# The first batch's 4x4 pixel sums as TensorE products with a matrix of ones

## The chip, the core and the metric

The kernel runs on one core of one Trainium2 chip. The metric is the device time of one execution in microseconds (us), as the median of several runs. The core has a matrix engine (TensorE, PE in the profile; its loads of weights have a row of their own, PEld), three engines for element-wise work (VectorE or DVE, ScalarE or ACT, GpSimd or POOL), and SyncE (SP), which here issues all DMAs.

## The reference

Two batches of keys and values come as images of 384 x 32 pixels with 128 channels. Windows of 4 x 4 pixels are averaged to 768 tokens a batch, which one 128 x 128 matrix projects; the result is both keys and values. Each of 2 x 12288 queries attends to its batch's 768 tokens, and the output goes through two MLPs of width 2048.

```python
kv_pool = kv.reshape(B, H // r, r, W // r, r, C).mean(axis=(2, 4))   # r = 4
kv_flat = kv_pool.reshape(B, -1, C) @ w_sr
k = v = kv_flat
s = scale * (q @ k.transpose(0, 2, 1))
s = s - s.max(-1, keepdims=True)
a = np.exp(s)
a /= a.sum(-1, keepdims=True) + 1e-09
x = a @ v                                  # attention
x = (h * cos(h)) @ w_out1                  # h = x @ w_in1
x = (g * sigmoid(1.702 * g)) @ w_out2      # g = x @ w_in2
```

## The kernel before

Queries go in units of 512 tokens (48 of them, in groups of 16), four steps of 128 tokens to a unit. For a group the attention steps come first, then the steps of the first MLP, then those of the second. The program is written out by hand: `at(step, rank, fn)` puts work into a step, and each engine runs its instructions in the order in which they are written. Nothing reorders them between engines; an engine waits on semaphores.

The change touches what stands ahead of the first step. SP issues the load of `w_sr`, then the keys of batch 0: six blocks j, each of four loads r (`kv_load`, L117 to L124), 24 loads of 256 KB, then two units of q (L304), then eight pieces of the first MLP's weights (L194). At most eight loads are under way; each further issue waits for the one eight before it.

Block j is 16 window rows of 8 windows: 128 windows, one on each partition. Load r brings pixel row r of every window, 4 pixels x 128 channels, 2 KB a partition. A load thus takes every fourth pixel row of 64, 16 pieces of 16 KB each.

`kv_pool` (L126 to L145) sums the 16 pixels of a window by halving adds over the free axis: three of 512 wide, one of 256, one of 128. GpSimd does blocks 0 and 3, VectorE 1, 2, 4 and 5 (L557 to L568). `kv_project` (L147 to L182) then takes half a batch, three blocks, in three stages. `turn` transposes the pooled blocks on TensorE (L155) into PSUM, and ScalarE copies them out with the factor 1/16 (L157). `keys` multiplies by `w_sr` (L161), and ScalarE and VectorE write the product as a high and a low part (L163, L164). `values` does the same the other way round (L176, L179, L180). `q_prep(0)` transposes the first queries (L312 to L317); it is called behind `turn` of the second half, ahead of that half's `keys`. The first scores (L345) need the keys of both halves and the queries.

Products of plain float32, as L161 and L176, are two instructions to a call, each with its load of weights; transposes and the products of the main loops (fp32r, L102 to L104, L345, L400) are one. In TensorE's rows the first operand to be held still is called the weights; the other one streams through.

Of the kernel before, what the change touches and what calls it, by code (L numbers as in the profile page):

```python
# [11 lines left out]
F32 = mybir.dt.float32  # L12
# [4 lines left out]
ALU = mybir.AluOpType  # L17
AX = mybir.AxisListType

P = 128  # L20
# [12 lines left out]
def tile_pooled_attention_two_mlps(  # L33
# [11 lines left out]
    nc = tc.nc  # L45
    B, N, C = q.shape
# [23 lines left out]
    make_identity(nc, ident)  # L70
    wsr = cp.tile([P, C], F32, tag="wsr", name="wsr")
    wi, wo = [None, None], [None, None]
    kT = [cp.tile([P, 2, 2, HK], F32R, tag=f"kT{b}", name=f"kT{b}") for b in range(B)]
# [10 lines left out]
    def acc(key=None):  # L84
        """The bank used longest ago; a key holds it until let_go."""
        a = banks.pop(0)
        if key is None:
            banks.append(a)
        else:
            held[key] = a  # L90
        return a
# [13 lines left out]

# [1 line left out]
    pooled, staged = {}, {}  # L107
    peak = cp.tile([P, 2 * B], F32, tag="peak", name="peak")

    def kv_place(b, j):  # L110
        """Two places' worth where each of three weights goes later."""
        if j % 2 == 0:
            tag = ("wi1", "wo1", "wo0")[j // 2]
            staged[b, tag] = cp.tile([P, 2, R, R * C], F32, tag=tag, name=f"kv{b}_{j}")
        return staged[b, ("wi1", "wo1", "wo0")[j // 2]][:, j % 2]

    def kv_load(b, j):  # L117
        t = staged[b, j] = kv_place(b, j)
        hh = P // (W // R)
        src = kv[b, j * hh * R : (j + 1) * hh * R].rearrange(  # L120
            "(h r) (w s) c -> r h w (s c)", r=R, s=R
        )
        for r in range(R):
            nc.sync.dma_start(t[:, r, :], src[r])  # L124

    def kv_pool(b, j, eng):  # L126
        """The sums over a tile's windows, as short operations."""
        f = staged.pop((b, j)).rearrange("p r x -> p (r x)")
        n = R * R * C // 2
        ops = []  # L130

        def add(o, x, y):
            ops.append(lambda: eng.tensor_tensor(o, x, y, op=ALU.add))

        while n > C:
            for i in range(0, n, UNIT):
                e = min(i + UNIT, n)
                add(f[:, i:e], f[:, i:e], f[:, n + i : n + e])
            n //= 2
        pj = f[:, :C]  # L140
        if j >= 4:
            pj = st.tile([P, C], F32, tag="pooled", name=f"pooled{b}_{j}", bufs=2)
        pooled[b, j] = pj
        add(pj, f[:, :n], f[:, n : 2 * n])
        return ops  # L145

    def kv_project(b, h):  # L147
        """Half of a batch's keys and values, as stages."""
        js = range(h * KC // 2, (h + 1) * KC // 2)
        v = {}  # L150

        def turn():
            tp = acc()
            for i, j in enumerate(js):
                nc.tensor.transpose(tp[:, i * P : (i + 1) * P], pooled.pop((b, j)), ident)  # L155
            pT = v["pT"] = fp.tile([P, HK], F32, tag="f", name=f"pT{b}_{h}")
            nc.scalar.activation(pT, tp[:, :HK], AF.Copy, scale=1.0 / (R * R))  # L157
# [25 lines left out]

# [1 line left out]
    PIECE = DFF // 8  # L185
# [17 lines left out]
    def w_split(m, part, k, raw):  # L203
        """Float32 words, then their two parts."""
        d = wi[m] if part == 0 else wo[m].rearrange("p h k c -> p h (k c)")
# [3 lines left out]
        def words(stage):  # L209
# [7 lines left out]
            w = v["w"] = word.bitcast(F32)  # L217
            # Sign and upper exponent bit keep their places; seven exponent bits and twenty
            # mantissa bits move up by three, and the lower word's upper bits follow.
            if stage == 0:  # L220
                nc.vector.tensor_scalar(
                    word, high, 3, 0x3FFFFFFF, op0=ALU.logical_shift_left, op1=ALU.bitwise_and
                )
                nc.vector.scalar_tensor_tensor(
                    word, high, 0xC0000000, word, op0=ALU.bitwise_and, op1=ALU.bitwise_or
                )
            elif stage == 1:
                nc.vector.scalar_tensor_tensor(  # L228
                    word, low, 29, word, op0=ALU.logical_shift_right, op1=ALU.bitwise_or
                )  # L230
                nc.vector.tensor_scalar(
                    high, high, 1, 28, op0=ALU.logical_shift_left, op1=ALU.logical_shift_right
                )
            else:
                # What lies below float32's normal range is zero.
                nc.vector.scalar_tensor_tensor(w, high, 7.0, w, op0=ALU.is_ge, op1=ALU.mult)
# [13 lines left out]
    def w_bound(flags):  # L250
        """1 where no |h| of the first MLP can come near pi / 2: |x_c| <= max |v_c|; as stages."""
        mags = [t.rearrange("p i x -> p (i x)") for t in parts_ring]
# [29 lines left out]

    # What outlives a branch stays in places of its own, used in turn.
    def ring(n, shape, dtype, name):
# [7 lines left out]

# [1 line left out]
    qn, qT = {}, {}  # L294
# [23 lines left out]

# [1 line left out]
    tasks = defaultdict(list)  # L320
# [15 lines left out]
    def attn_step(s, u, t):  # L336
# [53 lines left out]
        def pv(part):  # L390
# [10 lines left out]
            if t == QT - 1 and part == len(PV_CUTS) - 2:  # L401
                # Before the branch the scalar engine goes on to the next stage at once.
                if u != GROUP - 1:
                    keep(u)
# [31 lines left out]
    def mlp_step(s, m, u, p):  # L436
# [7 lines left out]
        def nonlinear():  # L444
# [7 lines left out]
            else:  # L452
                # Two parts of two pi, the first one's products exact; the ends as Sin takes them.
                k = fp.tile([P, 2, UNIT], I32, tag="f", name=f"k{u}_{p}")
# [71 lines left out]

    nc.vector.memset(half_pi, math.pi / 2)
    first = GROUP * QT
    eased = set()
# [13 lines left out]
    with tc.manual_schedule():  # L543
# [12 lines left out]

        def pool_now(j, eng):  # L557
            for op in kv_pool(0, j, eng):
                op()

        pool_now(0, nc.gpsimd)
        pool_now(1, nc.vector)
        pool_now(2, nc.vector)
        half0[0]()
        pool_now(3, nc.gpsimd)
        half0[1]()
        pool_now(4, nc.vector)
        pool_now(5, nc.vector)  # L568
        half0[2]()
        half1[0]()  # L570
        q_prep(0)
        half1[1]()
        half1[2]()
        late = [*range(4, KC), *range(4)]
        # Steps that don't also split queries on the same engine.
        free = [x for x in range(6, first) if x % QT != 1]
# [22 lines left out]
        for fn, step in zip(stages, (41, 42, 43, 44, 46, 47)):  # L599
            at(step, 58, fn)  # L600
        # The second MLP's inputs take the places of the first one's.
        x_ring = ring(GROUP, [P, UNIT], F32, "x")
        # Products of the next stage, where this one's last steps wait for each other.
        for i, rank in enumerate((21, 21, 70)):
# [57 lines left out]
```

## Time and profile before

| | us |
|---|---|
| median of 3 runs | 2772.45 |
| lowest and highest | 2771.88, 2774.81 |
| span of the profiled execution | 2771.1 |
| TensorE busy in it | 2733.8 (99%) |
| VectorE busy | 1914.3 (69%) |
| ScalarE busy | 2046.8 (74%) |
| GpSimd busy | 525.5 (19%) |

The profiled execution has its span alone on the page, from its first to its last instruction; the runs' times hold what lies around it too, 1.35 us by the median. Busy time counts an instruction from start to end; TensorE's instructions overlap, and their ends are modelled. A chain of waits is followed back from the last instruction, at each step to what released it. A wait that a row names in brackets is the idle time ahead of the instruction and what ended it.

### The profile page before, as it was taken

What the parts mean: (1) busy time and instruction counts of PE and PEld (TensorE: products, weight loads), DVE (VectorE), ACT (ScalarE), POOL (GpSimd) and SP (SyncE); (2) the same over time, 40 slices, a digit from 0 to 9 for tenths busy, and PEclk for the clock granted to TensorE, in tenths of its full rate; (3) what the DMA queues carried; (4) which work ended last, traced back from release to release, by engine and by line L of the source; (5) the groups of instructions that cost most, each with busy time, mean ns of one, the idle gap of its engine ahead of it and who ended that gap; (6) DMA issues with size and microseconds to landing.
All of it is one profiled execution on the core that took longest, in us unless ns stands there. A gap on an engine that the chain in (4) does not pass through costs nothing.

```text
span 2771.1 us, 35036 instructions
## 1 busy us (share of the span) xinstructions
PE 2733.8 (99%) x13680; PEld 2310.2 (83%) x13680; DVE 1914.3 (69%) x2201; ACT 2046.8 (74%) x2455; POOL 525.5 (19%) x430
## 2 busy tenths in 40 slices
PE   6999999999999999999999999999999999999999
PEld 5998888888888899888888888889998888888887
DVE  6988999864444577788886444457778888644444
ACT  4777888777777777777777777777777777777776
POOL 5852232000000144200000000014420000000000
PEclk9999999999999999999999999999999999999999
DMA  7210000000000000000000000000000000000000
GB/s 206 69 40 15 20 20 8 1 1 13 15 12 12 22 26 24 5 1 1 1 1 1 12 12 12 12 20 30 22 1 1 1 1 1 1 12 12 12 12 17
DMA packets 27710, 48.53 MB, mean 18 GB/s; under 512 B 2832, under 2 KB 7056, under 8 KB 27536
## 3 DMA queue, kind: packets, MB, share of 16 engines
q1 hardware_dynamic: 27536, 46.21, 5.3%
q8 instruction: 109, 1.79, 0.3%
q14 instruction: 65, 0.53, 0.1%
HBM read 33.62 MB, written 12.58 MB: 17 GB/s over the span
## 4 chain that ended last, share of the span: by engine, by line
PE 92%; DVE 6%; DMA 1%; ACT 0%; issue 0%; POOL 0%; SPq 0%; DVEq 0%; POOLq 0%; ACTq 0%
PE w L103 12%; PE w L102 12%; PE w L104 12%; PE a L102 12%; PE a L103 12%; PE a L104 12%; PE a L400 7%; PE w L345 7%; PE w L370 4%; DVE g L461 2%; DVE gs L468 2%; PE a L502 1%; DMA kv<-in_kv_dram 1%; PE a L312 1%; DVE wt L228 1%; DVE nm L352 0%
## 5 line engine op out<-in xcount | busy, mean ns | idle before, releaser
L468 DVE TENSOR_TENSOR gs<-g,gs 128x1024 fp32r<-128x1024 f32 x752 | 923.5, 1228 | 565.0 <-ACT gs L466 565.0
L466 ACT ACTIVATE gs<-g 128x1024 fp32r<-128x1024 f32 x768 | 807.0, 1051 | 4.0 <-PE a L104 2.5
L448 ACT ACTIVATE g<-w 128x1024 f32<-128x1024 f32 x384 | 394.1, 1026 | 300.7 <-PE w L104 300.7
L102 PE MATMUL w<-xs,wi 128*128 128x512 f32 x1536 | 613.1, 399 | 0.0
L103 PE MATMUL w<-xs,wi 128*128 128x512 f32 x1536 | 608.1, 396 | 0.0
L104 PE MATMUL w<-xs,wi 128*128 128x512 f32 x1536 | 607.5, 395 | 0.0
L103 PE MATMUL a<-gs,wo 128*128 128x512 f32 x1536 | 606.3, 395 | 0.0
L102 PE MATMUL a<-gs,wo 128*128 128x512 f32 x1536 | 604.8, 394 | 1.0 <-DVE gs L468 1.0
L104 PE MATMUL a<-gs,wo 128*128 128x512 f32 x1536 | 597.8, 389 | 0.0
L451 ACT ACTIVATE g<-w,half_pi 128x1024 f32<-128x1024 f32 x384 | 430.1, 1120 | 219.4 <-PE w L104 218.9
L461 DVE TENSOR_TENSOR g<-w,g 128x1024 f32<-128x1024 f32 x384 | 469.1, 1222 | 134.1 <-ACT g L451 134.0
L334 POOL TENSOR_TENSOR xs<-x,xs 128x512 fp32r<-128x512 f32 x96 | 176.5, 1839 | 1692.4 <-ACT xs L333 1601.2
L102 PEld LDWEIGHTS a<-gs,wo 128*128 128x128 f32 x1536 | 288.5, 188 | 72.9 <-DVE gs L468 2.3
L104 PEld LDWEIGHTS w<-xs,wi 128*128 128x128 f32 x1536 | 288.3, 188 | 70.8
L104 PEld LDWEIGHTS a<-gs,wo 128*128 128x128 f32 x1536 | 288.7, 188 | 66.6
L102 PEld LDWEIGHTS w<-xs,wi 128*128 128x128 f32 x1536 | 288.4, 188 | 66.9 <-DVE pT L388 0.4
L103 PEld LDWEIGHTS a<-gs,wo 128*128 128x128 f32 x1536 | 288.3, 188 | 65.5
L103 PEld LDWEIGHTS w<-xs,wi 128*128 128x128 f32 x1536 | 288.8, 188 | 62.2
L388 DVE TENSOR_TENSOR pT<-w,pT 128x768 fp32r<-128x768 f32 x192 | 183.6, 956 | 110.3 <-ACT pT L385 110.0
L385 ACT ACTIVATE pT<-w 128x768 fp32r<-128x768 f32 x192 | 156.2, 814 | 133.8 <-PE w L370 129.6
L345 PE MATMUL w<-kT,qT 128*128 128x384 f32 x1152 | 250.4, 353 | 1.3 <-DVE pT L388 1.3
L365 POOL TENSOR_SCALAR e<-e,rs 128x768 f32<-128x768 f32 x192 | 182.6, 951 | 348.2 <-DVE rs L364 190.1
(67 smaller groups left out, 2091.0 us busy)
## 6 DMA issues: line engine op xcount, KB each, us to landing
kv<-in_kv_dram SPq DMA_DIRECT2D x48, 256.0 KB, 4.9
qn<-in_q_dram SPq DMA_DIRECT2D x48, 256.0 KB, 2.6
out_dram<-r SPq DMA_DIRECT2D x48, 256.0 KB, 2.0
raw<-in_moe_w_in_dram SPq DMA_DIRECT2D x16, 256.0 KB, 4.5
raw<-in_moe_w_out_dram SPq DMA_DIRECT2D x16, 256.0 KB, 2.6
wsr<-in_w_sr_dram SPq DMA_DIRECT2D x1, 64.0 KB, 1.8
```

Of the source, the lines that this page charges most:

```text
L102: nc.tensor.matmul(o, wh, xl, start=start, stop=False)
L103: nc.tensor.matmul(o, wh, xh, start=False, stop=False)
L104: nc.tensor.matmul(o, wl, xh, start=False, stop=stop)
L345: nc.tensor.matmul(sc[:, h, :HK], w, kT[b][:, i, h], start=w is qh and i == 1, stop=w is ql,)
L365: nc.gpsimd.tensor_scalar(e, e, rs, 1.0, op0=ALU.mult, op1=ALU.mult)
L388: nc.vector.tensor_tensor(v["lo"], v["src"], f32(v["hi"]), op=ALU.subtract)
L400: nc.tensor.matmul(o, w, x, start=k == 0, stop=k == n - 1)
L448: nc.scalar.activation(g, h, AF.Gelu_apprx_sigmoid)
L451: nc.scalar.activation(g, h, AF.Sin, bias=half_pi)
L461: nc.vector.tensor_tensor(g, h, g, op=ALU.mult)
L466: nc.scalar.activation(gs[:, 0], g, AF.Copy)
L468: eng.tensor_tensor(gs[:, 1], g, f32(gs[:, 0]), op=ALU.subtract)
```

## The change

Batch 0's keys are loaded in another shape: load d (of 24) now takes 16 whole pixel rows, 256 KB that lie together. A partition (x, w) holds four neighbouring pixels of pixel row x, those of window w. So the 128 partitions of a load are 16 pixel rows x 8 windows across, which is 4 window rows of 8 windows, 32 windows.

`window` is a 128 x 32 matrix with a one where partition (x, w) belongs to the window: VectorE makes it from the identity by one reduction. `kv_sum` multiplies, for each of the four neighbouring pixels, the pixels (as weights, 128 partitions x 128 channels) by `window` and accumulates the four products in 32 columns of PSUM. These columns hold channels x windows, already turned, so batch 0 has no transposes any more and no adds. `kv_project(0, h)` calls it for 12 loads in `turn`. The second half's `turn` is now called behind `q_prep(0)`. Batch 1 is loaded and pooled as before.

```diff
+    window = cp.tile([P, P // R], F32, tag="window", name="window")
     def kv_load(b, j):
         t = staged[b, j] = kv_place(b, j)
+        if b == 0:
+            rows = kv[b].rearrange("(d x) (w s) c -> d x w (s c)", x=R * R, s=R)
+            for r in range(R):
+                nc.sync.dma_start(t[:, r, :], rows[j * R + r])
+            return
+    def kv_sum(h, d, a):
+        j, r = divmod(d, R)
+        f = staged[0, j][:, r, :]
+        n = P // R
+        o = a[:, (d - h * HK // n) * n :][:, :n]
+        for i in range(R):
+            nc.tensor.matmul(
+                o, f[:, i * C : (i + 1) * C], window, start=i == 0, stop=i == R - 1
+            )
         def turn():
             tp = acc()
-            for i, j in enumerate(js):
-                nc.tensor.transpose(tp[:, i * P : (i + 1) * P], pooled.pop((b, j)), ident)
+            if b == 0:
+                for d in range(js.start * R, js.stop * R):
+                    kv_sum(h, d, tp)
+            else:
+                for i, j in enumerate(js):
+                    nc.tensor.transpose(tp[:, i * P : (i + 1) * P], pooled.pop((b, j)), ident)
     nc.vector.memset(half_pi, math.pi / 2)
+    nc.vector.tensor_reduce(
+        window, ident.rearrange("p (h r w) -> p h w r", h=R, r=R), axis=AX.X, op=ALU.add
+    )
-        pool_now(0, nc.gpsimd)
-        pool_now(1, nc.vector)
-        pool_now(2, nc.vector)
         half0[0]()
-        pool_now(3, nc.gpsimd)
         half0[1]()
-        pool_now(4, nc.vector)
-        pool_now(5, nc.vector)
         half0[2]()
-        half1[0]()
         q_prep(0)
-        half1[1]()
-        half1[2]()
+        for stage in half1:
+            stage()
```

On TensorE, from its first instruction to the first scores, the order before is this. A row is the kernel's line, the instruction with what it writes and reads, the size, and how many calls follow each other; `kv_0`, `kv_2` and `kv_4` are blocks 0 and 1, 2 and 3, 4 and 5, `a_86` and `a_87` two banks of PSUM, and `qn_95` the first queries.

```order
L155 MATMUL a_86<-ident,kv_0_103 128x128 x2
L155 MATMUL a_86<-ident,kv_2_112 128x128
L161 MATMUL a_87<-pT_0_166,wsr 128x384
L176 MATMUL a_86<-wsr,pT_0_166 128x128 x3
L155 MATMUL a_87<-ident,kv_2_112 128x128
L155 MATMUL a_87<-ident,pooled_4_177 128x128
L155 MATMUL a_87<-ident,pooled_5_183 128x128
L312 MATMUL a_86<-ident,qn_95 128x128 x4
L161 MATMUL a_87<-pT_1_197,wsr 128x384
L176 MATMUL a_86<-wsr,pT_1_197 128x128 x3
L345 MATMUL w_83<-kT_79,qT_89 128x384 x6
```

The order after, at the same place. The lines are those of the changed kernel: L161 is now `kv_sum`, L183 and L198 the products of keys and values, L334 the queries' transposes, L367 the scores; the banks are `a_87` and `a_88`, the first queries `qn_96`.

```order
L161 MATMUL a_87<-window,kv_0_105 128x32 x32
L161 MATMUL a_87<-window,kv_2_114 128x32 x16
L183 MATMUL a_88<-pT_0_198,wsr 128x384
L198 MATMUL a_87<-wsr,pT_0_198 128x128 x3
L334 MATMUL a_88<-ident,qn_96 128x128 x4
L161 MATMUL a_87<-window,kv_2_114 128x32 x16
L161 MATMUL a_87<-window,kv_4_123 128x32 x32
L183 MATMUL a_88<-pT_1_265,wsr 128x384
L198 MATMUL a_87<-wsr,pT_1_265 128x128 x3
L367 MATMUL w_84<-kT_80,qT_90 128x384 x6
```

The three transposes of each half have become 48 sums, and the queries' transposes have moved from behind the second half's blocks to ahead of them.

On VectorE, from the start to the first scores' maximum, before:

```order
L527 MEMSET half_pi 128x1
L133 TENSOR_TENSOR kv_0_103<-kv_0_103 128x512 x3
L133 TENSOR_TENSOR kv_0_103<-kv_0_103 128x256
L133 TENSOR_TENSOR kv_0_103<-kv_0_103 128x128
L133 TENSOR_TENSOR kv_2_112<-kv_2_112 128x512 x3
L133 TENSOR_TENSOR kv_2_112<-kv_2_112 128x256
L133 TENSOR_TENSOR kv_2_112<-kv_2_112 128x128
L164 SCALAR_TENSOR_TENSOR kT_79<-a_87,kT_79 128x384
L167 TENSOR_REDUCE peak<-a_87 128x1
L133 TENSOR_TENSOR kv_4_121<-kv_4_121 128x512 x3
L133 TENSOR_TENSOR kv_4_121<-kv_4_121 128x256
L133 TENSOR_TENSOR pooled_4_177<-kv_4_121 128x128
```

And after, where L186, L189 and L202 are the low part of the keys, their peak and the low part of the values, and L374 the scores' maximum:

```order
L549 MEMSET half_pi 128x1
L550 TENSOR_REDUCE window<-ident 128x32
L186 SCALAR_TENSOR_TENSOR kT_80<-a_88,kT_80 128x384
L189 TENSOR_REDUCE peak<-a_88 128x1
L202 TENSOR_TENSOR vN_82<-a_87,vN_82 128x384
L186 SCALAR_TENSOR_TENSOR kT_80<-a_88,kT_80 128x384
L189 TENSOR_REDUCE peak<-a_88 128x1
L202 TENSOR_TENSOR vN_82<-a_87,vN_82 128x384
L374 TENSOR_REDUCE nm_0_308<-w_84 128x1
```

All adds (L133) are gone from this stretch, the reduction that makes `window` has come in, and the first values' low part (L180 before, where it stood behind the last of the adds) now follows the keys' peak.

## Rows read from the trace of the kernel before

**Rows 1.** The page: busy time and share of the span by engine; the last chain by engine.

```profile
PE 2733.8 (99%) x13680; PEld 2310.2 (83%) x13680; DVE 1914.3 (69%) x2201; ACT 2046.8 (74%) x2455; POOL 525.5 (19%) x430
...
PE 92%; DVE 6%; DMA 1%; ACT 0%; issue 0%; POOL 0%; SPq 0%; DVEq 0%; POOLq 0%; ACTq 0%
```

**Rows 2.** The chain of waits up to 75 us: start, length, what; longest pieces.

```profile
26.93 0.70 DVE kv L133
...
28.85 0.30 DVE pooled L133
...
29.20 0.47 PE a L155
29.67 1.11 PE a L312 x4
...
33.60 2.91 PE w L345 x12
...
45.56 1.05 PE w L345 x6
```

**Rows 3.** Groups by line and shape up to 31 us, of VectorE and of GpSimd.

```profile
L133 DVE TENSOR_TENSOR kv<-kv 128x512 f32<-128x512 f32 x12 | 9.0, 754 | 11.8 <-DMA kv<-in_kv_dram 11.5
...
L133 POOL TENSOR_TENSOR kv<-kv 128x512 f32<-128x512 f32 x6 | 7.5, 1260 | 11.4 <-DMA kv<-in_kv_dram 11.2
```

**Rows 4.** Timeline of TensorE: start, length from first start to last end, line, count.

```profile
18.76 1.65 PE L161 MATMUL a<-pT,wsr 128*128 128x384 f32 x2 [0.58 <-ACT pT L157]
20.20 1.49 PE L176 MATMUL a<-wsr,pT 128*128 128x128 f32 x6
24.27 0.47 PE L155 MATMUL a<-ident,kv 128*128 128x128 f32 x1 [2.58 <-POOL kv L133]
...
139.27 0.83 PE L176 MATMUL a<-wsr,pT 128*128 128x128 f32 x6
```

**Rows 5.** One line each: count, shortest, median and longest ns; 0 to 34 us, then later.

```profile
L161 PE MATMUL a<-pT,wsr x4: 847/848/1007, 18.8 to 31.2; 128*128 128x384 f32 x4
...
L176 PEld LDWEIGHTS a<-wsr,pT x12: 286/333/337, 19.6 to 33.0; 128*128 128x128 f32 x12
L176 PE MATMUL a<-wsr,pT x12: 421/421/580, 20.2 to 33.2; 128*128 128x128 f32 x12
...
L345 PE MATMUL w<-kT,qT x7: 333/338/443, 35.0 to 36.2; 128*128 128x384 f32 x7
...
L176 PEld LDWEIGHTS a<-wsr,pT x12: 187/192/192, 139.1 to 152.9; 128*128 128x128 f32 x12
L176 PE MATMUL a<-wsr,pT x12: 270/275/275, 139.3 to 153.0; 128*128 128x128 f32 x12
...
L269 PEld LDWEIGHTS a<-xs,vr x4: 80/81/82, 159.1 to 172.4; 128*2 128x2 f32 x4
...
L370 PE MATMUL w<-ident,e x339: 270/273/329, 59.8 to 228.0; 128*128 128x128 f32 x170
...
L102 PE MATMUL a<-gs,wo x48: 389/393/497, 2701.5 to 2764.1; 128*128 128x512 f32 x48
```

**Rows 6.** Stretches: busy time and count by engine, granted clock, DMA share, GB/s.

```profile
10.00:25.00 15.00, 4.82 (x12) 2.75 (x12) 9.63 (x16) 1.47 (x3) 8.36 (x8) 1.00 1.07 276
27.00:33.00 6.00, 3.81 (x12) 2.48 (x13) 2.88 (x6) 2.06 (x4) 1.02 (x1) 1.00 1.05 385
```

**Rows 7.** Us to landing of the first 24 key loads, then the first q loads (L304).

```profile
DMA to landing us min/median/max: 3.6/7.2/7.7
...
L304 SPq DMA_DIRECT2D qn<-in_q_dram x2: 334/336/337, 20.1 to 21.1; - x2
...
DMA to landing us min/median/max: 7.0/7.1/7.2
```

**Rows 8.** Timeline of ScalarE and of VectorE behind the mark.

```profile
29.70 0.49 ACT L157 ACTIVATE pT<-a 128x384 f32<-128x384 f32 x1 [7.49 <-PE a L155]
...
32.62 0.56 DVE L164 SCALAR_TENSOR_TENSOR kT<-a,kT 128x384 fp32r<-128x384 f32 x1 [3.01 <-ACT kT L163]
```

More of the change, by code (lines that the diff above doesn't have):

```diff
@@ L555, in tile_pooled_attention_two_mlps @@
         half0, half1 = kv_project(0, 0), kv_project(0, 1)
-        def pool_now(j, eng):
-            for op in kv_pool(0, j, eng):
-                op()
-        pool_now(0, nc.gpsimd)
-        pool_now(1, nc.vector)
-        pool_now(2, nc.vector)
         half0[0]()
-        pool_now(3, nc.gpsimd)
         half0[1]()
-        pool_now(4, nc.vector)
-        pool_now(5, nc.vector)
         half0[2]()
-        half1[0]()
         q_prep(0)
-        half1[1]()
-        half1[2]()
+        for stage in half1:
+            stage()
         late = [*range(4, KC), *range(4)]
```

## The prediction

> **What bounds the kernel now.** I read the page first: TensorE is busy 99% of the span and carries 92% of the chain that ended last [rows 1]. Behind the start lies one TensorE-bound stream, so a change at the start counts by when that stream begins and by nothing else. So I read next the chain of waits over the first 40 us [rows 2]. Up to 26.93 it is the DMA of batch 0's keys. Then come the last adds on VectorE, the last transpose at 29.20, the queries' transposes from 29.67, key and value products, and the scores from 33.60. I call 29.67, when the last pooled block has left TensorE, the **mark**. The question is where the mark goes and what follows it.
>
> **What is removed.** In the first 31 us VectorE makes 12 adds of 754 ns over 128x512, GpSimd 6 of 1260 ns [rows 3], with 14 smaller ones between them. Nearly all lie beside the DMA. On the path lie those after 26.93, until 29.15, and one transpose of 0.47 [rows 2]. If the DMA stays as it is, 29.67 - 26.93 = 2.7 us is all that can be won here.
>
> **What is added outside TensorE.** One VectorE reduction makes the matrix of ones, once. It reads 128x128 elements; an add over 128x512 takes 0.75 us [rows 3], so it takes less. It stands second on VectorE, and no key lands before 1.17 + 3.6 = 4.8 us at today's pace [rows 7]: nothing. Without that cover it would cost up to 0.75.
>
> **What is added on TensorE.** 24 loads of 4 pixels each make 96 calls. One call in float32 is two loads of weights and two products (the one call of L161 at 18.76 shows as x2, the three of L176 as x6 [rows 4]); so 192 pairs, 96 in each half. The pixels are the weights (128 columns), the ones stream through them (32 columns).
>
> No row has a pair with 32 streaming columns. The nearest is L176 with 128: early six take 1.49 us, one alone 0.421, (1.49 - 0.42) / 5 = 0.213 us a pair; near 139 us six take 0.83, one 0.275: 0.111 a pair [rows 4, 5]. These are the clock's two levels, 1.2 and 2.4 GHz. The granted clock reads 1.00 early too [rows 6], so in these first microseconds the durations are the witness. Load and product are equally wide there, so this row doesn't tell which sets the pace. Two others do: a load of 128 columns takes 188 ns fast, one of 2 columns 81 [rows 5], and the difference, 107, is nearly the whole fast pair; and a product of L102 that finds its load not yet made takes 497 instead of 393, 104 more [rows 5]. So the load sets it, and shrinking the product frees nothing. I take **0.213 us slow, 0.111 fast**. Bounds of the slow price: above, load and product in series, 0.213 + 0.213 / 4 = 0.267; below, the first product of L161 waits 1007 - 847 = 160 ns for its load [rows 5]; and lowest, if the clock were no matter to loads, the fast 0.111.
>
> The Trainium skill, page "TensorE: Matmul & The Clock Gate", section "LDWEIGHTS (loading the stationary operand)", gives a load its columns divided by 1.2, which is 107 ns for 128, and doesn't ask for the clock. The trace speaks against it: the same loads take 333 ns early and 192 late [rows 5]. By the page the sum below would end at about 2774 with the faster key loads.
>
> **What is moved.** TensorE runs in order. Its order is now: 12 loads' sums, the first half's keys and values, *the queries' transposes*, and only then the second half's 12 loads. So half the pairs stand behind the whole first half and behind q's landing: q is issued at 20.1 and lands 7.0 to 7.2 later, at 27.2 [rows 7]. On VectorE the first values' low part no longer stands behind two tiles of adds; nobody waited for it. On SP the order of issues is the same, but batch 1's first eight loads, which go where blocks 4 and 5 were, now wait for the last sums, and a q load stands behind them that is needed a stage later. That wait moves with the scores: no price of its own.
>
> **The loads themselves.** Each now reads one contiguous 256 KB, as the q loads do. Key loads move 276 GB/s (10 to 25 us), q and weight loads 385 (27 to 33) [rows 6]. If the shape is the reason, 256 KB take 0.68 us instead of 0.95, and q lands at 4.5 + 24 x 0.68 = 20.8. In my sum this is hidden: TensorE is later than either. First landing: 4.8 [rows 7] at today's shape, 4.5 taken.
>
> **The sum, slow clock.** Half 0: 4.5 + 96 x 0.213 = 24.9, with the first load and the drain 25.2. ScalarE's copy 0.53 with its start [rows 8], load 0.16, keys 2 x 0.64 = 1.28, values 6 x 0.213 = 1.28: 28.5. Queries 4 x 0.213 = 0.85: 29.3. Half 1: 96 x 0.213 = 20.4, drain 0.2: mark at **50.0**, 20.3 later. From the mark to the scores it was 33.60 - 29.67 = 3.9; without the queries it is copy 0.53, keys 0.16 + 1.28 + 0.21, copy 0.53, low part 0.63 [rows 8]: 3.4. Net 20.3 - 0.5 = +19.8. The profiled execution spans 2771.1; the runs' median is 2772.45, the 1.35 outside the span stay. 2772.45 + 19.8 = **2792**.
>
> **Rivals.**
> *A: the clock rises during the sums, and the loads are faster.* For it: TensorE is then fed without a gap, and an uninterrupted feed from 29.67 [rows 2] had L345 at its fast 338 ns from 35.25 on [rows 5], 5.6 us later. Against it: there 128 to 384 columns streamed each time; here the array streams for a quarter of each pair. And the feed of 18.76 to 21.69 did not raise it: the next transpose took 0.47, against 0.273 fast [rows 4, 5]. The time: 5.6 us do 26 pairs, 70 x 0.111 = 7.8, half 0 ends at 18.0, values at 20.0, q lands at 20.8, its transposes 0.45, 96 x 0.111 = 10.7: mark 32.1. On to the scores at fast durations (copies 0.53 twice, load 0.11, keys 0.64 + 0.2, low part 0.63) 2.6 instead of 3.9, and the first twelve score products 2.1 instead of 2.9 (six fast take 1.05 [rows 2]): 2.4 - 1.3 - 0.8 = +0.3, **2773**. The same page of the Trainium skill, Part 1 ("The HAM clock gate"), says that sustained matmul activity releases the clock; if these sums are such activity, it is this rival. No row of before shows whether they are.
> *B: the clock rises, the loads stay as they are.* q lands at 27.2, TensorE idles 7 us and is slow again: 28.1 + 5.6 + 7.8 = mark 41.5, scores at 44.1, less 0.8: +9.7, **2782**.
> *C: slow clock, cheaper loads of weights.* At 0.160 half 0 ends at 20.2, the queries at 24.3 to 28.1, mark 39.9 to 43.6, scores 43.3 to 47.0: +9.7 to +13.4, **2782 to 2786**. At 0.111: values 18.7, queries 21.7 to 28.1, mark 32.5 to 38.9, +2.3 to +8.7, **2775 to 2781**.
> *D: pairs in series.* 192 x 0.054 = 10.4 more: **2803**.
> *E: faster.* The sums' loads go at the price of a transpose's load: a fast transpose that finds it not yet made takes 329 instead of 273 ns [rows 5], 0.056. With fast clock and fast loads half 1 is 96 x 0.056 = 5.4 behind 21.3: mark 26.8, -2.9 - 1.3 - 0.8 = -5.0, **2767**. It begins to win from a pair of about 0.107 down and needs all three; the 104 ns of L102 speak against it.
> That the change doesn't do what it says is excluded by the order: the 96 calls are there, the adds are gone.
>
> **How the numbers follow.** Chances: forecast 0.46; A 0.23; B 0.07; C 0.09 and 0.05; D 0.06; E 0.04. Below about 0.2% (5.5 us) a measurement of this kernel can't tell a change. Slower: 0.46 + 0.07 + 0.09 + 0.06 and a part of C's cheaper price, 0.70. Same: A, the rest of that price, some of E, 0.27. Faster: the rest of E, 0.03. The forecast alone is good to 4 us (first landing 1, pair price 2, the clock's rise behind the mark 1): 2788 to 2796. The range reaches down to A, 2771 to 2796; D, E and A's lower edge are left out.
>
> **What would show it.** The sums' pairs 0.21 us apart (0.11: A); the queries' transposes near 29 (21: A); key loads at 385 or 276 GB/s; the last sum's end near 50, the scores from 53. An end of the sums before 35 makes the clock or the load's price wrong, one after 55 the overlap. If the mark comes as forecast and the end isn't 20 us later, the stream behind it had slack that the chain of waits doesn't show.

## The result and the profile after

The changed kernel takes 2789.78 us (median of 5 runs, 2788.25 to 2790.8), the kernel before 2773.96 in the same comparison (2771.88 to 2774.81): ratio 1.0061, 95% interval 1.0048 to 1.0073. It is slower by 16 us, and lies inside the range, 2 us from the forecast.

The page after, beside [rows 1]: the line of busy time by engine.

```profile
PE 2770.8 (99%) x13866; PEld 2349.4 (84%) x13866; DVE 1901.1 (68%) x2182; ACT 2047.5 (73%) x2455; POOL 516.7 (19%) x420
```

TensorE is still busy 99% of the span, of a span 17.6 us longer (2788.7 against 2771.1). It has 186 instructions more (192 products came, 6 transposes went) and is busy 37 us longer. VectorE and GpSimd have lost 13.2 and 8.8 us of work, of which only the last adds, 26.93 to 29.15 [rows 2], had been waited for.

The chain of waits after, over the first 70 us (start, length, what), to be read beside [rows 2]:

```profile
1.18 2.85 DMA kv<-in_kv_dram
...
4.17 20.67 PE a L161 x96
...
25.41 1.65 PE a L183 x2
...
27.05 1.28 PE a L198 x6
...
28.73 1.09 PE a L334 x4
29.82 20.38 PE a L161 x96
...
53.70 2.90 PE w L367 x12
```

The DMA is on it for the first load only. From 4.17 on TensorE is the chain: 96 pairs, the first half's keys and values, the queries, 96 pairs, then the scores at 53.70 where [rows 2] had them at 33.60. The mark is at 50.20. (A chain has an instruction begin where the one before it ends, a timeline has its own start: the first scores stand at 53.70 in the one and at 53.35 in the other.) Before, the DMA set the start, with TensorE busy 5.3 of the first 27 us; after, TensorE does, and the DMA engines are nearly idle by then (a share of 0.05 from 30 to 50 us).

The groups by line and shape over the first 52 us (count | busy us, mean ns of one | idle before):

```profile
L161 PE MATMUL a<-window,kv 128*128 128x32 f32 x192 | 41.2, 400 | 4.2 <-DMA kv<-in_kv_dram 4.2
L161 PEld LDWEIGHTS a<-window,kv 128*128 128x128 f32 x192 | 41.1, 333 | 4.2 <-issue 4.1
```

A load of weights takes 333 ns, as the early loads of L176 did by their median [rows 5], though a quarter of the columns stream here. The pair's pace is (20.67 - 0.40) / 95 = 0.213 us. The loads follow each other without a gap (PEld is busy 10.00 of 10.00 us in the next row).

A stretch of the trace after (from:to and length, busy time and count of PE, PEld, DVE, ACT, POOL, then granted clock, DMA share, GB/s), beside [rows 6]:

```profile
10.00:20.00 10.00, 10.00 (x49) 10.00 (x48) 0.00 (x0) 0.00 (x0) 0.00 (x0) 1.00 1.05 389
```

Key loads now move 389 GB/s instead of 276. The granted clock reads 1.00 here, as it does early in the trace of before, where loads of the same length ran; so the durations are the witness, and they are those of the 1.2 GHz level. The record first shows a change of the clock at 35.2 us before and at 55.3 after.

### The profile page after: what moved, and what is told of

Same layout as the page of the kernel before. It is cut to its first block, busy times and chain, and to the rows that moved or that the text cites. A ratio compares the mean times of both kernels' runs of the same rounds, so it can differ in the third digit from the quotient of the medians.

```text
span 2788.7 us, 35369 instructions
## 1 busy us (share of the span) xinstructions
PE 2770.8 (99%) x13866; PEld 2349.4 (84%) x13866; DVE 1901.1 (68%) x2182; ACT 2047.5 (73%) x2455; POOL 516.7 (19%) x420
## 4 chain that ended last, share of the span: by engine, by line
PE 94%; DVE 5%; ACT 0%; POOL 0%; issue 0%; DMA 0%; SPq 0%; POOLq 0%; DVEq 0%; ACTq 0%
PE w L103 12%; PE w L104 12%; PE w L105 12%; PE a L103 12%; PE a L104 12%; PE a L105 12%; PE a L422 7%; PE w L367 7%; PE w L392 4%; PE a L161 1%; DVE g L483 1%; DVE gs L490 1%; PE a L524 1%; PE a L334 1%; DVE wt L250 1%
## 5 line engine op out<-in xcount | busy, mean ns | idle before, releaser
L367 PE MATMUL w<-kT,qT 128*128 128x384 f32 x1152 | 249.5, 352 | 0.0
```

Source lines behind the costliest of these rows:

```text
L367: nc.tensor.matmul(sc[:, h, :HK], w, kT[b][:, i, h], start=w is qh and i == 1, stop=w is ql,)
```

## The experiments

The theory: the cost is the weight loads' price at the slow clock, 192 x 0.213 us, of which 20 us lie on the path. The rivals: the order (queries ahead of the second half), the clock alone, the loads' new shape. All kernels below are the changed kernel with the edit that is shown; `...` stands for code left out. A time from one run alone is called so, and there the trace carries the argument. The kernel before, run beside them, had medians of 2772.2 to 2772.8 us.

### The old order

```diff
+        half1[0]()
         q_prep(0)
-        for stage in half1:
-            stage()
+        half1[1]()
+        half1[2]()
```

> The queries' transposes go back behind the second half's sums, as in the kernel before; nothing else differs. Theory (192 pairs at 0.213 one behind the other set the start, wherever q stands): the second half's sums start near 28.4 instead of 29.6 and end near 49, the queries' transposes then lie ahead of the keys, the scores come within 1 us of 53.3 and the time stays within 2 us of 2790. Rival (what costs is that the second half was put behind q): back to about 2774.

2790.34 us (one run). Its timeline of TensorE (start, length, line, count, idle before):

```profile
28.60 20.69 PE L161 MATMUL a<-window,kv 128*128 128x32 f32 x96 [0.35 <-DVE peak L189]
49.10 1.09 PE L334 MATMUL a<-ident,qn 128*128 128x128 f32 x4
```

The second half begins 1 us earlier and the scores come at 52.68 instead of 53.35. The order costs a microsecond at most; it is not the cause.

### Half the products

```diff
-        for i in range(R):
+        for i in range(2):
...
-                o, f[:, i * C : (i + 1) * C], window, start=i == 0, stop=i == R - 1
+                o, f[:, i * C : (i + 1) * C], window, start=i == 0, stop=i == 1
```

> Only two of the four pixels of each row are multiplied: 48 pairs a half instead of 96; half of each sum is left out. Theory: each half's sums take 10.2 us instead of 20.5; the first ends near 14.5, the queries wait for q until about 21.5, the second half runs from 22.3 to 32.7: 17.5 us earlier than with all pixels, the time near 2772. Rival (the stream behind the start has slack that swallows most of the delay): much less than 15 us gained.

2773.33 us, ratio 1.0002 (0.9993 to 1.0011). TensorE's timeline:

```profile
3.99 10.57 PE L161 MATMUL a<-window,kv 128*128 128x32 f32 x48 [3.99 <-DMA kv<-in_kv_dram]
...
21.31 1.08 PE L334 MATMUL a<-ident,qn 128*128 128x128 f32 x4 [3.24 <-DMA qn<-in_q_dram]
22.19 10.29 PE L161 MATMUL a<-window,kv 128*128 128x32 f32 x48
```

Half the pairs take half the time, 10.4 us a half. The kernel's time is back at that of the kernel before, so the loss goes with the number of pairs. What is new is the wait of 3.24 us for q: with less work ahead of it, the order of the changed kernel begins to cost.

### The clock: ones repeated to 128 columns

```diff
-    window = cp.tile([P, P // R], F32, tag="window", name="window")
+    window = cp.tile([P, P], F32, tag="window", name="window")
-        o = a[:, (d - h * HK // n) * n :][:, :n]
+        o = a[:, (d - h * HK // n) * n :][:, :P]
```

The reduction that makes `window` is made four times, side by side. Each product now writes 128 columns of PSUM, and the 96 that are too many are written over by the next loads' sums or not read.

> The ones are repeated to 128 columns, so each product streams 128 columns instead of 32; the pixels' loads of weights stay as they are. Theory (a pair costs its load of weights, 0.213 us at the slow clock, and the clock stays slow because the array streams only a quarter of the time): the pairs begin at 0.213 as before, load and product being equally wide, but the array now streams without a gap, so some 5.6 us after the first sum the pairs fall to 0.111, the last sum ends near 32 instead of 50 and the time is near 2772. Rival (the clock doesn't rise for such sums however wide they stream): 0.213 throughout, 2790. Rival (product and load one after the other): the pairs get longer, to 0.37, and the time goes above 2815.

2775.12 us, ratio 1.0009 (1.0000 to 1.0019): four times the streaming makes it 15 us faster. TensorE's timeline, and then a stretch of it (columns as above, the granted clock third from the end):

```profile
4.06 13.20 PE L161 MATMUL a<-window,kv 128*128 128x128 f32 x96 [4.06 <-DMA kv<-in_kv_dram]
...
22.70 1.08 PE L334 MATMUL a<-ident,qn 128*128 128x128 f32 x4 [3.29 <-DMA qn<-in_q_dram]
23.58 11.95 PE L161 MATMUL a<-window,kv 128*128 128x128 f32 x96
```

```profile
22.70:25.50 2.80, 2.79 (x13) 2.80 (x14) 0.00 (x0) 1.08 (x2) 0.51 (x1) 0.50 1.05 379
```

The first half takes 13.2 us instead of 20.7: its first pairs are 0.213 us apart, those after 8.75 us 0.112. So the clock does rise while the array streams 128 columns to each load, and with 32 it did not in 41 us. The time came out 3 us later than expected, because TensorE waited 3.29 us for q; behind that wait the granted clock is 0.50 (1.2 GHz) until 25.8, and the second half's first pairs are slow with it.

The wide ones with the old order of the queries settle that:

> The ones repeated to 128 columns, as in the wide run, and the queries' transposes behind the second half's sums. Theory (the wide run lost 3.3 us waiting for q, and its clock with that wait): without the wait the clock stays up, the second half's 96 pairs take 0.1116 us each, 10.7 us, from about 20.4; sums end near 31, scores near 34 instead of 38.2, about 2771. Rival (the clock falls again between the halves, or while the second half runs): second half's sums 12 us or more, scores 36 or later, 2773 to 2775.

2770.96 us, ratio 0.9995 (0.9986 to 1.0004).

```profile
19.59 10.98 PE L161 MATMUL a<-window,kv 128*128 128x128 f32 x96 [0.97 <-DVE peak L189]
```

The second half now runs at the fast level from end to end, (10.98 - 0.27) / 95 = 0.113 us a pair. (In this execution the clock also rose at 7.09 us and not at 8.75, which is worth 0.8 us in the first half.) The scores come at 32.88, a little ahead of the 34 expected; the time is as expected. With the clock up and the old order, sums on TensorE take as long as the adds did.

### The clock: warmed up, then 32 columns

```diff
+        dummy = sp.tile([P, UNIT], F32, tag="t", name="dummy", bufs=3)
+        nc.vector.memset(dummy, 0.5)
+        for k in range(5):
+            nc.tensor.matmul(pw[k % 3][:, 0], ident, dummy, start=True, stop=True)
         half0[0]()
```

> Five products of 512 streaming columns of a constant tile are added ahead of the first sum (some 7 us from 2 on, results unused); the sums are as in the change, 32 columns wide. The clock is then fast when the sums begin. Theory (streaming a quarter of the time doesn't count as much as streaming all the time): the first sums are 0.111 apart, then the clock falls back to slow within some us although TensorE is fed without a gap, and the second half runs at 0.213; last sum between 43 and 54, time 2783 to 2794. Rival (a feed of loads and short products keeps a clock that is up): 0.111 until the first half's end near 19, a fall at most where q is waited for, last sum near 33 to 38, time 2774 to 2779.

2788.41 us (one run). Four stretches (columns as above):

```profile
5.20:11.80 6.60, 6.60 (x45) 5.17 (x44) 0.00 (x0) 0.00 (x0) 0.00 (x0) 1.00 0.98 365
12.00:28.00 16.00, 15.28 (x66) 14.24 (x66) 0.86 (x2) 1.08 (x3) 0.00 (x0) 0.50 0.97 357
29.00:32.30 3.30, 3.30 (x32) 3.27 (x30) 0.00 (x0) 1.09 (x2) 1.26 (x1) 1.00 0.28 79
33.00:46.00 13.00, 13.00 (x63) 13.00 (x62) 0.00 (x0) 0.00 (x0) 0.00 (x0) 0.50 0.00 1
```

The sums begin at 7.67 at the fast level, and though TensorE is fed without a gap the clock is at 0.50 from 12 us on. Behind the queries' transposes it is up again (30 pairs begin in 3.3 us), and falls again under the sums (61 in 13.0). So rival A failed on its condition: these sums neither raised the clock nor held it. In the changed kernel the same keys, values and transposes, 25.41 to 29.82, left the clock where it was; why they raised it here and not there is open. Part 1 of the page "TensorE: Matmul & The Clock Gate" of the Trainium skill ("The HAM clock gate") says that sustained matmul activity releases the clock. The trace agrees for 128 streaming columns (fast from 8.75 us) and not for 32 (0.50 from 12 to 28 us).

### The old shape of the loads

`kv_load` without its new branch, so that the sums are taken over other pixels.

```diff
-        if b == 0:
-            rows = kv[b].rearrange("(d x) (w s) c -> d x w (s c)", x=R * R, s=R)
-            for r in range(R):
-                nc.sync.dma_start(t[:, r, :], rows[j * R + r])
-            return
```

> Only the loads' shape is undone: each takes 16 pieces of 16 KB at 64 KB distance again, so the pixels land in other partitions and each sum is over the wrong pixels; all instructions and their order are the change's. Theory (TensorE is later than either shape): the time stays within 2 us of 2790, the last sum within 1 us of 50. On the loads themselves: if the shape is the reason for their pace, key loads fall from 387 to about 276 GB/s though no other engine reads or writes the memory beside them; if the adds on VectorE and GpSimd were the reason, they stay near 387.

2791.94 us (one run). The stretch of its key loads (columns as above):

```profile
10.00:20.00 10.00, 10.00 (x49) 10.00 (x48) 0.00 (x0) 0.00 (x0) 0.00 (x0) 1.00 1.05 285
```

285 GB/s with VectorE and GpSimd idle, where the changed kernel has 389: the shape is the reason, 16 pieces of 16 KB against 256 KB that lie together. It costs little here only because the loads are hidden behind the sums (the first one lands 0.8 us later, and the scores come 0.8 us later, at 54.17).

### Weights of 64 columns

Each call is split in two, each with half of the 128 channels as weights and half of the output partitions.

```diff
-            nc.tensor.matmul(
-                o, f[:, i * C : (i + 1) * C], window, start=i == 0, stop=i == R - 1
-            )
+            for z in range(2):
+                nc.tensor.matmul(
+                    o[z * 64 : (z + 1) * 64], f[:, i * C + z * 64 : i * C + (z + 1) * 64], window,
+                    start=i == 0, stop=i == R - 1,
+                )
```

> Each call is made as two, with 64 columns of weights each: 384 pairs of half-size loads, the same sums. Theory (a pair costs its load, and a load its columns): a pair takes about 0.107 us at the slow clock, the 192 pairs of a half again some 20.5 us, the time stays within 4 us of 2790. Rival (0.213 is a fixed price of a pair, as a wait of one accumulating product for the one before it in the same PSUM columns): 41 us a half, the time near 2831.

2774.09 us (one run): neither answer. Twice the instructions take half the time. TensorE's timeline:

```profile
7.16 8.75 PE L162 MATMUL a<-window,kv 128*64 128x32 f32 x160 [1.02 <-DMA kv<-in_kv_dram]
...
22.36 1.08 PE L336 MATMUL a<-ident,qn 128*128 128x128 f32 x4 [2.93 <-DMA qn<-in_q_dram]
23.37 10.46 PE L162 MATMUL a<-window,kv 128*64 128x32 f32 x192
```

A half takes 10.5 us, (10.46 - 0.29) / 191 = 0.053 us a pair at the slow clock. In the trace the pairs start in twos, 0.007 us apart, and 0.107 us from one two to the next. So a load of 64 columns costs half of one of 128, and two loads for different halves of the output run side by side. The page "TensorEngine Tiling (Array Packing)" of the Trainium skill, section "Tiling Modes", says that "Tiles operate independently: Different tiles can execute LdWeights and Matmul in parallel", and this trace agrees, by 20.7 us against 10.5.

With the queries behind the second half, where they don't make TensorE wait:

> The split in two with 64 weight columns, and the queries' transposes behind the second half's sums, so that they no longer wait for q (2.93 us idle in the split alone, which took 2774.1). Theory (0.85 us a load, TensorE never waits for q): half 0 ends near 14.5, values near 17.8, half 1 near 28, scores near 31.4, 2768 to 2770. Rival (the order was not what held it, the idle time comes back at another place): scores stay near 37, 2774.

2770.40 us, ratio 0.9990 (0.9981 to 0.9999), 0.4 us above what the theory had. The profiled execution is one of two (of 11) that took about 2765 and not 2770, and its second half shows why.

```profile
19.59 4.85 PE L162 MATMUL a<-window,kv 128*64 128x32 f32 x150 [0.36 <-DVE peak L191]
24.69 1.41 PE L162 MATMUL a<-window,kv 128*64 128x32 f32 x42 [0.24 <-issue]
```

150 pairs in 4.85 us are 0.032 each, against 0.053 at the slow clock: in this execution the clock rose during the sums, at 20.14. What decides whether it does was not tried.

### Weights of 32 columns

The same split in four, queries behind the second half.

> Each call of the sums is split in four with 32 weight columns each, which write 32 partitions of the result each; the queries' transposes go behind the second half's sums, as in the run with the old order. Theory (all four column quarters of the array load and run side by side, a load's price going with its columns): two quarters' width gave pairs 0.0533 us apart, so four give 0.0133 us, a load of 256 KB costs 32 x 0.0133 = 0.43 us, less than the 0.68 us in which one lands, and TensorE waits for the DMA: sums end near 21, scores near 24.6, three us before those of the kernel with adds on VectorE and GpSimd (27.6, 2764.3): about 2761.5. Rival 1 (only two parts run side by side, the price still goes with the columns): pairs 0.027 us apart, 0.85 us a load, TensorE-bound, sums end near 28, scores near 31.4, 2768 to 2770. Rival 2 (the pair has a fixed least price, 0.053 us): 1.7 us a load, sums end near 49, scores near 53, about 2790.

2774.74 us, ratio 1.0010 (1.0001 to 1.0019); 13 us over the theory, and by neither of the rivals. TensorE's timeline:

```profile
13.26 1.93 PE L162 MATMUL a<-window,kv 128*32 128x32 f32 x128 [2.97 <-issue]
18.63 0.69 PE L162 MATMUL a<-window,kv 128*32 128x32 f32 x33 [3.44 <-issue]
...
23.19 1.40 PE L162 MATMUL a<-window,kv 128*32 128x32 f32 x86 [0.36 <-DVE peak L191]
25.74 1.94 PE L162 MATMUL a<-window,kv 128*32 128x32 f32 x128 [1.16 <-issue]
29.47 1.94 PE L162 MATMUL a<-window,kv 128*32 128x32 f32 x128 [1.79 <-issue]
32.92 0.80 PE L162 MATMUL a<-window,kv 128*32 128x32 f32 x42 [1.52 <-issue]
```

The first part of the theory holds: four run side by side, 128 pairs in 1.93 us, 0.015 each with the last one's length in it. But from the gap of 2.97 us on TensorE stands still after each 128 pairs, which are 256 instructions, 1.2 to 3.4 us for nothing that the timeline shows. Between the gaps of 3.44 and 1.16 there lie 33 + 2 + 6 + 86 = 127 pairs, the keys' and values' among them, so it is the number of instructions and not the sums that sets the place. The five gaps add up to 10.9 us. The queue that the profile calls "instruction" moves a packet of 16 KB about once for each such block: here its line in the DMA queues' view of the first gap, 10.29 to 13.25 (packets, MB, share of 16 engines).

```profile
q8 instruction: 1, 0.02, 2.2%
```

Each gap has its packet. By the trace the packets begin at 10.78, 16.22, 23.12, 26.86 and 30.59, and TensorE goes on at 13.26, 18.63, 25.74, 29.47 and 32.92, every time 2.3 to 2.6 us behind its packet's start. The split in two with the old order fits too: its one gap of 0.24 us ends at 24.69, and a packet begins at 22.28. In the two longest gaps the packet begins 0.5 and 1.0 us after TensorE has stopped, with key loads moving 392 and 381 GB/s beside it; in the other three it begins 0.8 to 1.5 us before. That TensorE waits there for its own instructions is what these rows fit; no run took the fetch alone away. The page "Runtime: NRT & Kernel Launch" of the Trainium skill, section "Instruction fetch mechanics", has instructions come in blocks of 256 and calls the cost of crossing into the next one mostly hidden. The 256 agree with the trace; hidden it is not, at 1.2 to 3.4 us a block.

### Fewer products: sums on VectorE

Neighbouring pixels are now added ahead of TensorE, which then makes fewer calls for each load. In all three kernels the queries stand in the old order, the adds for the second half stand between the stages of the first, and the reduction that makes `window` stands a few lines further down; the code below shows the sums alone. First all four are summed, by one strided reduction a load on VectorE (128x512 to 128x128):

```diff
+        nc.vector.tensor_reduce(near[d], f, axis=AX.X, op=ALU.add)
...
-        for i in range(R):
-            nc.tensor.matmul(
-                o, f[:, i * C : (i + 1) * C], window, start=i == 0, stop=i == R - 1
-            )
+        nc.tensor.matmul(o, f, window, start=True, stop=True)
```

> VectorE first adds the four neighbouring pixels of a load with one reduction of 128x512 (0.6 us, against a landing every 0.68), and TensorE multiplies only the sum: one call, two pairs, a load of keys instead of eight; the second half's sums stand ahead of the queries again. Theory: two pairs at 0.213 are 0.43 us a load, less than the 0.68 between landings, so the sums end about 1 us behind the last landing (20.7), near 22.3; scores near 26 instead of 53.3 and 33.3 before; the time 2763 to 2767, under both kernels. Rival (TensorE's pairs are dearer in gaps, or VectorE falls behind): sums end after 27, 2771 or more.

2769.46 us, ratio 0.9988 (0.9979 to 0.9997). The one line's statistics (shortest/median/longest ns), then the chain of waits:

```profile
L171 DVE TENSOR_REDUCE near<-kv x24: 1005/1011/1030, 3.9 to 26.7; 128x128 f32<-128x512 f32 x24
```

```profile
7.08 13.14 DVE near L171 x14
...
21.14 6.53 DVE near L171 x7
```

The reduction takes 1.01 us and not 0.6, so 24 of them are longer than the loads, and VectorE is the chain. Two contiguous adds (128x256, 128x128) instead, every fourth load's on GpSimd:

```diff
+        eng = nc.gpsimd if d % 4 == 1 else nc.vector
+        for n in (2 * C, C):
+            eng.tensor_tensor(f[:, :n], f[:, :n], f[:, n : 2 * n], op=ALU.add)
```

> As e4_hybrid, with the four neighbours added by two contiguous adds (128x256, 128x128; 0.43 and 0.29 us) instead of one strided reduction (1.01), every fourth load on GpSimd. Theory: 0.72 us on VectorE for three of four loads and 1.87 on GpSimd for the fourth keep up with a landing every 0.68, TensorE's two pairs take 0.43; the sums end near 22.2 instead of 28.3, the scores begin near 26 instead of 31.8, the time is 2762 to 2766. Rival (the stream behind the start gives back what starts earlier, as it gave back 2.5 of the change's 20): 2767 or more.

2764.31 us, ratio 0.9970 (0.9959 to 0.9981): faster than both kernels. Its chain of waits:

```profile
14.39 4.13 DMA kv<-in_kv_dram
18.52 5.31 PE a L162 x24
23.84 0.91 PE a L343 x4
...
27.56 2.20 PE w L376 x12
```

Up to 18.52 the chain names the DMA, then the second half's 24 pairs; scores at 27.56 against 33.60 [rows 2]. The pairs ended 1.6 us later than expected (23.8 for 22.2). What released their first load of weights was not a landing but VectorE, which had just read the first half's keys' product (timeline of TensorE's loads of weights):

```profile
18.50 5.20 PEld L162 LDWEIGHTS a<-window,kv 128*128 128x128 f32 x24 [0.65 <-DVE peak L198]
```

Last, one add a load, and TensorE sums the remaining two pixels with weights of 64 columns:

```diff
+        nc.vector.tensor_tensor(f[:, : 2 * C], f[:, : 2 * C], f[:, 2 * C :], op=ALU.add)
...
+        for i in range(2):
+            for z in range(2):
+                nc.tensor.matmul(
+                    o[z * 64 : (z + 1) * 64], f[:, i * C + z * 64 : i * C + (z + 1) * 64], window,
+                    start=i == 0, stop=i == 1,
+                )
```

> VectorE makes one add over 128x256 per load (pixels 0 and 1 plus pixels 2 and 3), TensorE sums the two halves that are left in calls split in two with 64 weight columns each; queries' transposes behind the second half's sums. So a load costs VectorE 0.43 us and TensorE 8 x 0.0533 = 0.43 us, both less than the 0.68 us in which one lands, and GpSimd does nothing; the whole takes 384 instructions of TensorE for the sums, where the split in four took 1536 and waited for its instructions. Theory (the start is now bound by the DMA, with one add and one load's sums behind the last landing): sums end at 20.4 + 0.43 + 0.43, near 21.3, scores near 24.7, 2.8 us before the kernel with two adds (27.56, 2764.3): 2761 to 2762. Rival 1 (TensorE's instructions come late here too, gaps of 1 to 3 us ahead of the sums' end): scores 26 to 28, 2763 to 2765. Rival 2 (what is won ahead of 27.6 us is lost again behind it, to the DMA of batch 1's keys and of the weights): scores near 24.7, time as with the two adds, 2764.

2763.47 us, ratio 0.9966 (0.9954 to 0.9979), the fastest of all, though not told apart from the one before it.

```profile
7.52 6.71 PE L164 MATMUL a<-window,kv 128*64 128x32 f32 x80 [1.51 <-DVE kv L175]
...
18.11 5.34 PE L164 MATMUL a<-window,kv 128*64 128x32 f32 x96 [0.36 <-DVE peak L201]
23.38 1.12 PE L346 MATMUL a<-ident,qn 128*128 128x128 f32 x4
```

There are no late instructions. Up to 14.2 TensorE waits for the DMA, as expected; but the second half's sums begin at 18.11 only, since they stand behind the first half's keys and values and then wait for VectorE to have read the keys' product (its peak, L201), and they end at 23.4 instead of 21.3. The scores come at 26.97 by the timeline, 27.32 by the chain.

## Why the prediction was right, and where not

- **What bounds the start.** Right. The scores came 20.1 us later and the profiled span grew by 17.6; the run with half the pairs was 16.5 us faster again, back at the time of before.
- **The pair's price.** Right: 0.213 us in both halves, from the second pair to the last. Its bounds, 0.160 and 0.267, were too wide on both sides. The Trainium skill's 107 ns for a load of 128 columns (page "TensorE: Matmul & The Clock Gate", section "LDWEIGHTS (loading the stationary operand)") doesn't hold for these float32 loads at the slow clock, where the pair takes twice that; at the fast clock a pair takes 0.113.
- **The rivals.** A and B fell with the clock, which stayed at its lower level; C and D with the pair's price, which is the forecast's; E needed the fast clock and a cheaper pair. Where A's condition was met, with the wide ones, the time was 2775 for A's 2773: q came later than A's 20.8, and the clock fell in the wait for it.
- **The steps.** First sum 4.17, behind a landing at 4.03 (4.5 forecast for both), half 0 done 24.84 (25.2), values 28.33 (28.5), queries 29.82 (29.3; they waited 0.40 of issue), mark 50.20 (50.0), mark to scores 3.5 (3.4), scores +20.1 (+19.8).
- **The loads.** Right: 389 GB/s, by their shape, and hidden.
- **`window`.** Right: it took 0.38 us at 1.34, long before the first landing.
- **A count.** Between the 18 wide adds of [rows 3] lie 12 smaller ones (8 on VectorE, 4 on GpSimd), not 14. Nothing hangs on it.
- **The order.** The prediction gave it no price of its own in the forecast, and the run with the old order agrees (under 1 us). In its rivals q's landing did set a wait, and those runs show it: 2.9 to 3.3 us, wherever the first half ended early.
- **The step that was mis-sized: the end.** +19.8 was carried unchanged from the scores to the last instruction. It arrived as +17.6 in the span and about +16 in the medians. Behind the scores 2.5 us of their delay came back, in steps, and the largest can be read. The rest of the way from 17.6 to 16 lies in which executions were profiled. A run's time is 1.8 us longer than its span throughout, so before's, with 2771.1, lies 1.1 us under its median, and after's, with 2788.7, 0.7 over. So the forecast missed the change by 4 us of 20, and came within 2 us of the time partly by luck, since the median of before, with two more runs, stands 1.5 us above the 2772.45 that it started from.

ScalarE's exponentials run a constant 20.1 us behind those of before, to the 25th; the 26th is 18.8 behind. There TensorE of before waits, and TensorE of after doesn't. The kernel before, then after (timeline of TensorE, same place of the program):

```profile
105.89 0.82 PE L370 MATMUL w<-ident,e 128*128 128x128 f32 x6
107.88 1.31 PE L345 MATMUL w<-kT,qT 128*128 128x384 f32 x6 [1.17 <-DVE pT L388]
```

```profile
126.03 0.82 PE L392 MATMUL w<-ident,e 128*128 128x128 f32 x6
126.65 1.32 PE L367 MATMUL w<-kT,qT 128*128 128x384 f32 x6
```

VectorE's timeline of before, ahead of that wait, and the same three instructions after:

```profile
104.25 0.95 DVE L221 TENSOR_SCALAR wt<-raw 128x256 uint32<-128x256 uint32 x1 [0.30 <-issue]
105.23 1.39 DVE L224 SCALAR_TENSOR_TENSOR wt<-raw,wt 128x256 uint32<-128x256 uint32 x1
106.54 0.41 DVE L236 SCALAR_TENSOR_TENSOR wt<-raw,wt 128x256 f32<-128x256 uint32 x1
```

```profile
124.01 0.29 DVE L243 TENSOR_SCALAR wt<-raw 128x256 uint32<-128x256 uint32 x1
124.34 0.43 DVE L246 SCALAR_TENSOR_TENSOR wt<-raw,wt 128x256 uint32<-128x256 uint32 x1
124.68 1.05 DVE L258 SCALAR_TENSOR_TENSOR wt<-raw,wt 128x256 f32<-128x256 uint32 x1
```

Three steps of the weights' preparation took 2.70 us in the profiled execution of before and 1.72 after, and before they also began 0.37 us later beside the exponentials, 0.30 of it the wait in the first row: 1.35 us in all. The traces of all the other kernels regain the same at this place, whether their scores came earlier or later. So it is not slack in the stream but 1.35 us that the one profiled execution of before lost.

What goes with slow steps can be read from the traces, though no run took GpSimd's work away. Beside the slow ones GpSimd is at an add of batch 1's keys, or comes to one before they end (from 105.01, 1.32 us, before; from 125.43, 1.45 us, after, where it meets the third step). The trace of before has 160 such steps over 128x256 words. Of the 38 that begin while GpSimd is inside an instruction with two tensors as input, 34 take longer than the usual 0.3 or 0.4 us; of the other 122, 8 do. After, it is 31 of 35 and 8 of 125, and the other twelve traces have the same pattern. Which steps meet such an instruction differs from trace to trace; what that costs TensorE was read at this one place. Whether every execution of before loses the 1.35 us isn't known. The other 1.2 us come back in steps of 0.34 and less and in a slow drift, without a place that could be named.

## What to carry to other kernels

A sum made by TensorE with the data as weights costs a load of weights for every 128 columns of data, and a load's price goes with its own columns and the clock, not with how little streams through it: count loads, not flops, and count them at the clock that the stretch will really have. Moving work onto the engine that bounds the kernel pays only where that engine idles now, and only as much as fits into that idle time: with one add left on VectorE and 192 cheaper pairs in place of 192 dear ones, the same idea is 9 us faster than before instead of 16 slower. Look in the trace for whatever else runs in the stretch at the time you mean to fill: here q's landing, the reading of the keys' product and, as far as the packets tell, the supply of instructions each took over as soon as the bound ahead of them was gone.

## What the runs showed of the hardware that was not expected

- Loads of weights for different column parts of the array run side by side: pairs 0.213 us apart with 128 weight columns, 0.053 with two parts of 64, under 0.015 with four of 32, all at the slow clock. The same sums cost 20.7, 10.5 and about 6 us a half, the gaps not counted.
- In the split in four, TensorE stopped for 1.2 to 3.4 us after every 256 instructions, and went on 2.3 to 2.6 us after a packet of the instruction queue had begun.
- In these runs sums with 32 streaming columns to a load of 128 left the clock at 1.2 GHz for both halves, 41 us of pairs, and it fell from 2.4 GHz under them where it was up; with 128 streaming columns it rose. With two parts of 64 weight columns it rose in the profiled execution.
- Key loads of 16 pieces of 16 KB moved 285 GB/s, of 256 KB that lie together 389.
- One strided reduction over 128x512 to 128x128 took 1.01 us on VectorE; the two contiguous adds that do the same took 0.43 and 0.29.
- VectorE's steps over 128x256 words took 0.3 to 0.4 us alone and up to 1.4 us in the stretch shown beside GpSimd's adds of two tensors.
